# A 36-column tile placed in a dead tile's buffer, and the addresses behind it, in a decoder forward and backward kernel

## The chip, the cores and the metric

The kernel runs on one core of a Trainium2 chip. Its time is the device time of one execution in microseconds (us). Three runs gave 1169.02 us in the median (1167.36 to 1169.89).

## The reference

Four layers are applied to a residual vector `x` of two rows (batch 2, one decode position, width 1024): attention against a cache, an MLP, then the same two again with the same weights. The kernel returns the result and the gradients with respect to `x`, both caches, `wq`, `wo`, `w1`, `b1`, `w2` and `b2`.

```python
def _A_ref(x, k_cache, v_cache, wq, wo):        # 32 query heads, 4 kv heads, 16384 positions, head size 128
    ...
    q = (x @ wq).reshape(B, Sq, Hq, Dh).transpose(0, 2, 1, 3)
    k = jnp.repeat(k_cache, rep, axis=1)
    v = jnp.repeat(v_cache, rep, axis=1)
    p = _softmax(jnp.einsum("bhqd,bhkd->bhqk", q, k) * (Dh ** -0.5), axis=-1)
    o = jnp.einsum("bhqk,bhkd->bhqd", p, v)
    return o.transpose(0, 2, 1, 3).reshape(B, Sq, Hq * Dh) @ wo

def _B_ref(x, w1, b1, w2, b2):                   # 1024 -> 3584 -> 1024
    h = _gelu(jnp.einsum("bsd,df->bsf", _layernorm(x), w1) + b1)
    return jnp.einsum("bsf,fd->bsd", h, w2) + b2

x = x + _A_ref(_layernorm(x), k_cache, v_cache, wq, wo)
x = x + _B_ref(_layernorm(x), w1, b1, w2, b2)
x = x + _A_ref(_layernorm(x), k_cache, v_cache, wq, wo)
x = x + _B_ref(_layernorm(x), w1, b1, w2, b2)
...
_out, _vjp = jax.vjp(_f, A_x, A_k_cache, A_v_cache, A_wq, A_wo, B_w1, B_b1, B_w2, B_b2)
```

All inputs and outputs are bfloat16. Each cache is 2 x 4 x 16384 x 128, which is 32 MiB.

## The kernel before

The program is written as a list of pieces (`emit`), in an order fixed by hand; `Program.run` (lines 106 to 138) goes through the list and, ahead of each piece, gives free buffers to the next loads in the order of their first use. Nothing else schedules: each engine takes its instructions in the order in which the pieces issue them.

The buffers are 15 tiles called `slot0` to `slot14` (line 273), each of 128 partitions x 4096 bfloat16, so 8,192 bytes in every partition. Layer 1's tiles `e1` and `ds1` lend further buffers of the same size until they are needed for themselves. One load (`ld_kv` line 320, `ld_rows` line 325) fills one buffer, mostly 1 MiB, and is issued from SyncE's queue. A piece of a cache is 8,192 contiguous bytes in each partition; a piece of `wq`, `wo` or `w2` is four runs of 2,048 bytes; a row of `w1` is one run of 7,168 bytes.

The forward pass of both attention layers reads K and V, the backward pass of layer 1 reads them again, and so does that of layer 0. K and V blocks are turned on VectorE by 32 x 32 transposes of pairs of bfloat16 taken as int32 (line 482, into the tile `kT`) and multiplied on TensorE (lines 495 and 520). Until the backward pass of layer 0 begins at some 700 us, hardly anything is written to memory. From there on the gradients of the caches and of the weights are made as outer products (lines 1180 and 1234), cast from PSUM into halves or wholes of the slots on ScalarE (line 236) or VectorE (line 239), and stored from GpSimd's queue (lines 1185 and 1260), while K and V are still being read.

On-chip memory is taken from pools one behind the other: `const`, `vec`, `wrk`, `small`, `ktp`, `xp`, `bkp`, `pers` (lines 191 to 198). Within a pool each name takes its size rounded up to 32 bytes, times its buffers, in the order of first use. `dbias` is the last name in `wrk`, so its 144 bytes, rounded to 160, lie ahead of everything in the five pools behind: the small vectors of `small`, `kT`, `xt`, `blk`, `e0`, `e1`, `ds1`, `ds0`, `X0`, `X1` and the slots.

`dbias()` (lines 1266 to 1280) makes the gradients of `b1` and `b2`. It sums the four columns of `dh_all` and `gM_all` into the 28 + 8 columns of the tile `dbias` (lines 1271 and 1272), turns that on TensorE (line 1274), copies the rows into a half slot (line 1275) and stores them (lines 1277 and 1278). It is one piece among the background pieces of the last backward pass.

`g_a` is a tile of the same pool with two buffers of 128 x 56 float32. `gelu` takes one for each layer (line 828) and reads it last in line 848.

Of the kernel before, what the change touches and what calls it, by code (L numbers as in the profile page):

```python
# [9 lines left out]
F32 = mybir.dt.float32  # L10
# [131 lines left out]
def kernel(  # L142
# [27 lines left out]
    PE = nc.tensor  # L170
# [8 lines left out]
    DJ = D // 128  # L179
    FJ = F // 128  # L180
# [12 lines left out]
    wrk = ctx.enter_context(tc.tile_pool(name="wrk", bufs=2))  # L193
# [13 lines left out]
    def flat(t):  # L207
        return t.rearrange("p a b -> p (a b)")
# [5 lines left out]
    def ob():  # L214
        st["ob"] += 1
        return obanks[st["ob"] % 3]
# [25 lines left out]
    def dve(us):  # L242
        load_of("dve", us)
# [4 lines left out]
    identf = const.tile([128, 128], F32, name="identf")  # L248
# [1017 lines left out]
    def dbias():  # L1266
        c = P.chunk(kind="half")

        def f():
            s = wrk.tile([128, FJ + DJ], F32, name="dbias", bufs=1)  # L1270
            V.tensor_reduce(out=s[:, 0:FJ], in_=dh_all[:], axis=AX.X, op=ALU.add)
            V.tensor_reduce(out=s[:, FJ:], in_=gM_all[:], axis=AX.X, op=ALU.add)
            ps = ob()[0:FJ + DJ, 0:128]
            PE.transpose(ps, s[:], identf[:])
            V.tensor_copy(out=c.ap[0:FJ + DJ, 0:128], in_=ps)
            dve(0.7)
            GP.dma_start(out_7.rearrange("(j p) -> j p", p=128), c.ap[0:FJ, 0:128])
            GP.dma_start(out_9.rearrange("(j p) -> j p", p=128), c.ap[FJ:FJ + DJ, 0:128])

        return [(f, [c])]  # L1280
# [258 lines left out]
```

## Time and profile before

One execution was profiled. Its own time was 1169.38 us, its span from the first to the last instruction 1167.6 us.

| what | value |
|---|---|
| time of three runs, median | 1169.02 us |
| the profiled execution, time / span | 1169.38 us / 1167.6 us |
| mean granted TensorE clock | 0.862 |
| TensorE busy | 830.9 us (71%) |
| TensorE weight loads busy | 621.6 us (53%) |
| VectorE busy | 770.4 us (66%) |
| ScalarE busy | 488.8 us (42%) |
| GpSimd busy | 183.4 us (16%) |
| read from / written to HBM | 356.54 MB / 98.62 MB |
| both, over the span | 390 GB/s |

Busy time of an engine is the time in which one of its instructions ran. The DMA share is the time that packets took on the core's 16 DMA engines, divided by 16 times the stretch; packets of one engine may overlap a little, so it can be above 1. The trace also holds each DMA packet with its queue, size, start and duration. A packet here is one run of bytes moved by one DMA engine, and its duration is in whole ns. PEclk is the share of its full speed that TensorE was granted.

### The profile page before, as it was taken

What the parts mean: (1) busy time and instruction counts of PE and PEld (TensorE: products, weight loads), DVE (VectorE), ACT (ScalarE), POOL (GpSimd) and SP (SyncE); (2) the same over time, 40 slices, a digit from 0 to 9 for tenths busy, and PEclk for the clock granted to TensorE, in tenths of its full rate; (3) what the DMA queues carried; (4) which work ended last, traced back from release to release, by engine and by line L of the source; (5) the groups of instructions that cost most, each with busy time, mean ns of one, the idle gap of its engine ahead of it and who ended that gap; (6) DMA issues with size and microseconds to landing.
All of it is one profiled execution on the core that took longest, in us unless ns stands there. A gap on an engine that the chain in (4) does not pass through costs nothing. (4 is left out here: it accounts for less than half of the span.)

```text
span 1167.6 us, 34350 instructions
## 1 busy us (share of the span) xinstructions
PE 830.9 (71%) x14751; PEld 621.6 (53%) x14761; DVE 770.4 (66%) x1490; ACT 488.8 (42%) x1128; POOL 183.4 (16%) x578
## 2 busy tenths in 40 slices
PE   5665565457886546888777578879666987798875
PEld 4554564456775445777767465444333444444443
DVE  5764673269886536664656465979566977787875
ACT  0422223002423221244444206758455866676773
POOL 1000000010000000110111101423222332333341
PEclk9999999999999555577877657989887989798997
DMA  9999999989999999999999997999999999999995
GB/s 356 412 414 414 413 420 410 405 319 413 410 414 414 414 399 356 405 414 412 409 414 412 377 341 275 340 405 424 401 358 407 420 415 381 425 421 399 392 419 218
DMA packets 99636, 457.37 MB, mean 392 GB/s; under 512 B 7668, under 2 KB 11778, under 8 KB 60188
## 3 DMA queue, kind: packets, MB, share of 16 engines
q1 hardware_dynamic: 81660, 356.56, 76.6%
q0 software_dynamic: 17824, 98.63, 20.7%
q8 instruction: 115, 1.88, 0.6%
q14 instruction: 37, 0.30, 0.1%
HBM read 356.54 MB, written 98.62 MB: 390 GB/s over the span
## 5 line engine op out<-in xcount | busy, mean ns | idle before, releaser
L482 DVE STREAM_TRANSPOSE kT<-slot 128x512 int32<-128x512 int32 x480 | 322.3, 694 | 130.3 <-PE sc L495 91.1
L495 PE MATMUL sc<-qbd,kT 128*128 128x32 bf16 x4096 | 264.7, 223 | 14.4 <-DVE kT L482 11.2
L495 PEld LDWEIGHTS <-kT 128*128 128x128 bf16 x4096 | 210.5, 115 | 59.1 <-issue 27.1
L520 PEld LDWEIGHTS <-slot 128*128 128x128 bf16 x3648 | 148.4, 103 | 131.7 <-issue 48.7
L236 ACT CAST slot<-sc 128x512 bf16<-128x512 f32 x332 | 189.0, 593 | 66.2 <-PE sc L1234 32.5
L520 PE MATMUL sb<-xt,slot 128*128 128x8 bf16 x3648 | 165.9, 177 | 65.3 <-DMA slot<-in_A_v_cache_dram 28.9
L239 DVE CAST slot<-sc 128x512 bf16<-128x512 f32 x187 | 126.2, 681 | 37.2 <-PE sc L1180 18.8
L1180 PE MATMUL sc<-slot,blk 128*128 128x512 bf16 x335 | 129.6, 405 | 25.7 <-DVE slot L239 8.4
L711 ACT ACTIVATE e<-sc 128x512 bf16<-128x512 f32 x32 | 19.0, 597 | 253.9 <-DVE sc L708 182.1
L236 ACT CAST slot<-sb 128x512 bf16<-128x512 f32 x169 | 100.0, 592 | 47.6 <-PE sb L1180 27.0
L530 POOL COPY xt<-ds 32x64 int32<-32x64 int32 x368 | 84.7, 230 | 192.1 <-DVE ds L980 155.9
L402 ACT COPY slot<-tp 128x512 int32<-128x512 int32 x96 | 55.2, 586 | 139.8 <-PE tp L399 138.3
L399 PE MATMUL tp<-ident,slot 128*128 128x128 bf16 x832 | 81.4, 264 | 18.0 <-DMA slot<-in_A_wq_dram 12.0
L1180 PEld LDWEIGHTS <-blk 128*128 128x128 bf16 x512 | 45.0, 99 | 69.4 <-issue 57.3
L1180 PE MATMUL sb<-slot,blk 128*128 128x512 bf16 x170 | 68.8, 405 | 17.8 <-DVE slot L239 13.1
L399 PEld LDWEIGHTS <-slot 128*128 128x128 bf16 x832 | 66.9, 121 | 21.9 <-DMA slot<-in_A_wq_dram 12.8
L530 ACT COPY xt<-e 32x128 int32<-32x128 int32 x256 | 75.6, 295 | 3.9
L239 DVE CAST slot<-sb 128x512 bf16<-128x512 f32 x96 | 65.0, 677 | 16.6 <-DMA out_dram<-slot 7.1
L1185 POOL DMA_DIRECT2D out_dram<-slot x64 | 35.3, 551 | 215.7 <-ACT slot L236 178.8
L384 DVE STREAM_TRANSPOSE slot<-slot 128x1024 int32<-128x1024 int32 (+1 forms) x48 | 55.2, 1178 | 15.3 <-DMA slot<-in_A_wq_dram 8.1
L1234 PE MATMUL sc<-slot,X 128*128 128x512 bf16 x157 | 60.7, 407 | 5.5 <-DVE slot L239 3.3
L587 POOL TENSOR_TENSOR m_rstd<-ln_vpe,neghalf 128x2 f32<-128x2 f32 x2 | 1.4, 716 | 374.2 <-DVE ln_vpe L585 374.2
(282 smaller groups left out, 932.9 us busy)
## 6 DMA issues: line engine op xcount, KB each, us to landing
slot<-in_A_k_cache_dram SPq DMA_DIRECT2D x114, 1024.0 KB, 14.4
slot<-in_A_v_cache_dram SPq DMA_DIRECT2D x109, 1024.0 KB, 13.4
out_dram<-slot POOLq DMA_DIRECT2D x64, 1024.0 KB, 11.3
slot<-in_A_wq_dram SPq DMA_DIRECT2D x31, 1024.0 KB, 12.5
slot<-in_A_wo_dram SPq DMA_DIRECT2D x27, 1024.0 KB, 12.5
out_dram<-slot POOLq DMA_DIRECT2D x54, 512.0 KB, 12.5
slot<-in_B_w_dram SPq DMA_DIRECT2D x22, 896.0 KB, 11.0
slot<-in_B_w_dram SPq DMA_DIRECT2D x11, 1024.0 KB, 11.4
```

What stands on the lines that cost most here:

```text
L236: S.copy(out=dst, in_=src)
L239: V.tensor_copy(out=dst, in_=src)
L384: V.transpose(out=t.ap[:, h * nw * 256:(h + 1) * nw * 256].bitcast(I32).rearrange("p (w j m) -> p w j m", j=4, m=32), in_=c.ap[:, 0:4 * nc ...
L399: PE.transpose(tp[:, j * 128:(j + 1) * 128], c.ap[:, off + j * 128:off + (j + 1) * 128], ident[:])
L402: S.copy(out=d.bitcast(I32), in_=tp.bitcast(I32))
L482: V.transpose(out=kT[:].bitcast(I32).rearrange("p (w j m) -> p w j m", w=4, j=4), in_=c.ap[:, (i % 4) * 1024:(i % 4 + 1) * 1024].bitcast(I ...
L495: PE.matmul(sc[:, a0:a0 + 4, :, 2 * (i % 4) + q], lhsT=kv[:, 2 * q + w, :, e], rhs=qbd[:, g, 2 * w + e], start=(w == 0 and e == 0), stop=( ...
L520: PE.matmul(acc, lhsT=c.ap[:, n * 128:(n + 1) * 128], rhs=xv[:, i // 4, t // 2, :, 2 * (i % 4) + t % 2], start=(fresh and i == 0 and t == ...
L530: (GP.tensor_copy if on[t % len(on)] == "g" else S.copy)(out=d[32 * t:32 * t + 32, c0:c0 + cn, j, :], in_=s[32 * j:32 * j + 32, c0:c0 + cn ...
L1180: PE.matmul(ps, lhsT=hold["blk"][:, j, :], rhs=flat(qm(w)[:, (u % 2) * 4:(u % 2) * 4 + 4, :]), start=True, stop=True)
L1185: GP.dma_start((dKv if w == 0 else dVv)[g, :, c * 32:(c + 1) * 32, :], stg.ap.rearrange("p (t d) -> p t d", d=128))
L1234: PE.matmul(ps, lhsT=hold[j // 4 * 4][:, j % 4, :], rhs=Y.ap[:, y_at + c0:y_at + c0 + cn], start=True, stop=True)
```

## The change

The sums are written into a buffer of `g_a` in place of a tile of their own. The buffer has 56 columns, of which the first 36 are used.

```diff
         def f():
-            s = wrk.tile([128, FJ + DJ], F32, name="dbias", bufs=1)
+            s = flat(wrk.tile([128, FJ, 2], F32, name="g_a")[:])[:, 0:FJ + DJ]
             V.tensor_reduce(out=s[:, 0:FJ], in_=dh_all[:], axis=AX.X, op=ALU.add)
             V.tensor_reduce(out=s[:, FJ:], in_=gM_all[:], axis=AX.X, op=ALU.add)
             ps = ob()[0:FJ + DJ, 0:128]
-            PE.transpose(ps, s[:], identf[:])
+            PE.transpose(ps, s, identf[:])
```

The instructions, their order on every engine, their waits and their shapes stay as they were; two VectorE instructions and one TensorE instruction name another tile. With the tile `dbias` gone, everything in the pools behind `wrk` begins 160 bytes lower in each partition:

| tile | byte address before | after |
|---|---|---|
| `kT` (first of 3) | 36,000 = 70 x 512 + 160 | 35,840 = 70 x 512 |
| `xt` (first of 2) | 42,144 = 82 x 512 + 160 | 41,984 = 82 x 512 |
| `e0` | 49,312 = 96 x 512 + 160 | 49,152 = 96 x 512 |
| `ds1` | 82,080 = 160 x 512 + 160 | 81,920 = 160 x 512 |
| `slot0` | 104,608 = 204 x 512 + 160 | 104,448 = 204 x 512 |
| `slot14` | 219,296 = 428 x 512 + 160 | 219,136 = 428 x 512 |

All of `kT`, `xt`, `blk`, `e0`, `e1`, `ds1`, `ds0`, `X0`, `X1` and the slots had the remainder 160 and now have none. The pools `const`, `vec` and the rest of `wrk` stay in place.

## The prediction

> **What bounds the kernel now.** I read the page's slices first: is one resource full from end to end?
>
> ```profile
> DMA  9999999989999999999999997999999999999995
> GB/s 356 412 414 414 413 420 410 405 319 413 410 414 414 414 399 356 405 414 412 409 414 412 377 341 275 340 405 424 401 358 407 420 415 381 425 421 399 392 419 218
> DMA packets 99636, 457.37 MB, mean 392 GB/s; under 512 B 7668, under 2 KB 11778, under 8 KB 60188
> ...
> q1 hardware_dynamic: 81660, 356.56, 76.6%
> q0 software_dynamic: 17824, 98.63, 20.7%
> ```
>
> It is: the DMA engines are busy in nine tenths or more of almost every slice, and the two data queues fill 76.6 + 20.7 = 97.3% of the span. TensorE with 71% and VectorE with 66% have room. Second, the busy time by stretches: three stages that only load, the long last stage that loads and stores, and two short pure samples.
>
> ```profile
> core 0: us, PE busy (x) PEld busy (x) DVE busy (x) ACT busy (x) POOL busy (x), PEclk, DMA share, GB/s
> 29.00:204.00 175.00, 106.38 (x2252) 92.64 (x2250) 107.32 (x218) 48.52 (x145) 0.00 (x0) 1.00 1.02 414
> 262.00:437.00 175.00, 118.53 (x2575) 105.04 (x2576) 122.11 (x256) 47.35 (x144) 2.42 (x9) 0.85 1.02 412
> 467.00:642.00 175.00, 137.11 (x3076) 130.36 (x3074) 101.58 (x190) 72.07 (x191) 25.80 (x112) 0.74 1.02 411
> ...
> 758.00:1138.00 380.00, 303.14 (x3537) 161.91 (x3542) 289.75 (x496) 253.03 (x505) 121.77 (x354) 0.90 1.00 405
> ...
> 783.00:812.00 29.00, 26.92 (x309) 15.05 (x311) 23.91 (x42) 22.79 (x44) 8.51 (x24) 0.93 1.01 424
> 145.00:175.00 30.00, 19.96 (x424) 17.80 (x424) 20.73 (x44) 7.02 (x20) 0.00 (x0) 1.00 1.01 420
> ```
>
> The three load stages (525 us together) hold DMA at a share of 1.02 and reach 411 to 414 GB/s; where loads and stores mix, the same engines reach 424 at a share of 1.01. So time in the load stages is the time of DMA packets, and packets there are a little dearer than they need be. Third, the packets themselves, from the trace's records of size and duration. Loads of 8,192 bytes last 309 ns at the least; in the three load stages only some 10% of them do, the mean is 315.2, 315.3 and 315.8 ns and the 90th percentile 320. Loads of 2,048 bytes last 84 ns at the least, 88.0, 88.1 and 87.5 in the mean, 93 or 92 at the 90th percentile. From 758 to 1138 us, 89% of the 8,192-byte loads and 97% of the 2,048-byte ones are at 309 and 84 ns, and 91% of the 8,192-byte stores too.
>
> **The change part by part.** *The moved sums.* The four instructions of the piece that name the tile:
>
> ```profile
> L1271 DVE TENSOR_REDUCE dbias<-dh_all x1: 247/247/247, 829.1 to 829.1; 128x28 f32<-128x112 bf16 x1
> L1272 DVE TENSOR_REDUCE dbias<-gM_all x1: 164/164/164, 829.3 to 829.3; 128x8 f32<-128x32 bf16 x1
> L1274 PEld LDWEIGHTS sc<-identf,dbias x1: 96/96/96, 829.5 to 829.5; 128*36 128x36 f32 x1
> L1274 PE MATMUL sc<-identf,dbias x1: 287/287/287, 829.5 to 829.5; 128*36 128x128 f32 x1
> ```
>
> They stay with the same shapes. A wait for the old user of `g_a` could be new, but `gelu` read it last at 231.9 us (layer 0) and 449.5 us (layer 1), and the sums come at 829.1: cost nothing. Were that cover gone, the 247 + 164 ns of VectorE would be late by as much as the wait, with the K/V transposes of line 482 queued behind.
>
> *The engines' operands.* `kT`, `xt`, `e`, `ds` and the slots are read and written at new addresses by every engine. Does an engine mind where in a block of 512 bytes it begins? Line 420 answers from the trace of before, since its reads begin 160 or 416 and its writes 160, 288, 416 or 32 bytes behind a multiple of 512:
>
> ```profile
> L420 DVE STREAM_TRANSPOSE slot<-slot x28: 601/603/665, 424.7 to 454.8; 128x448 int32<-128x448 int32 x28
> L420 DVE STREAM_TRANSPOSE ds<-slot x4: 596/602/603, 425.2 to 441.0; 128x448 int32<-128x448 int32 x4
> ```
>
> A median of 603 ns with a least of 601 over all these starts: VectorE does not mind, and I put zero for it and for ScalarE and TensorE. These engines would also be covered: the load stages use 106 to 137 of 175 us of TensorE.
>
> *The transfers.* Every large load ends in a moved tile and every large store begins in one. No packet of before has a start at a multiple of 512 in these tiles, so I bound the price. The upper end of the gain within the observed packets: all that lies over the least duration goes. In the three load stages that is 20,790 packets of 8,192 bytes by 315.4 - 309 = 6.4 ns and 19,531 of 2,048 bytes by 87.9 - 84 = 3.9 ns, on 16 engines: 8.3 + 4.8 = 13.1 us. The lower end is a loss: packets could get as slow as the slowest tenth is now, 4.6 ns and 5.1 ns more: 6.0 + 6.2 = 12.2 us. Zero lies between. I take a gain, since a partial block at both ends of each 8,192-byte run is the one thing that the change removes, and the excess is per packet rather than per byte (6.4 ns on 8,192 bytes, 3.9 ns on a quarter of that), as a cost of a packet's ends would be. Not all of 13.1 us lands, because packets overlap: 525 us at 1.02 are 535.5 us of packet time; less 13.1 it is 522.4, and at the share of the mixed sample, 1.01, that takes 517 us. The gain is 8 us. The other 640 us get none: in the mixed stage loads are at the least already, and the tail from 1138 us is at a DMA share of 0.56.
>
> *The sum:* 0 + 0 - 8 against the profiled 1169.4 us: 1161 us, between 1156 (all 13.1) and 1167. That execution stands 0.4 us over the median of the three runs, so 1161 is against 1169.0 as well. What goes missing in the load stages arrives at the end whole only if SyncE finds free slots that much sooner; its largest waits before loads are for the turns,
>
> ```profile
> SPq L320 <- DVE kT L482: 177.5, 53, 11.8
> SPq L320 <- PE sc L495: 81.8, 28, 10.2
> ```
>
> and these waits lie ahead of transfers that land 13 to 14 us after their issue, so the queue is ahead of the engines and follows them when they get data earlier.
>
> **The rivals.** *B, the least duration falls too.* Packet times fit bytes plus a fixed part: (309 - 159) ns for 4,096 bytes more is 36.6 ns per 1,000 bytes, which leaves 9 ns of each 8,192-byte packet, 9 of a 4,096-byte store (159) and 9 of 2,048 bytes (84). If 160 bytes' worth of it, 5.9 ns, comes from the bytes before the start within an aligned block, then 99,636 - 7,668 = 91,968 packets by 5.9 ns on 16 engines are 33.9 us, of which some 31 would land (most stages are full): 1138 us. Against it: the 4-byte semaphore packets last 9 ns too, and their size has no room for it. Also, the 2,048-byte packets that carry eight rows of 256 bytes of `ident`, which starts 128 bytes behind a multiple of 256, last 84 ns in most cases, as one run of 2,048 does; eight starts cost no more than one. [...]
>
> *C, no change.* The excess over 309 ns comes from the HBM side of a stage that only reads. For it: the same slots at the same addresses take loads at 309 ns in 89% of cases as soon as stores run beside them, so the address alone isn't enough for an excess. Then all terms are zero: 1169 us.
>
> *D, slower.* The same term with the other sign: runs that all begin at the same place of a block meet in the on-chip memory's write side, where only loads press (the three load stages). Price as above, from the mean towards the 90th percentile, 12.2 us if all packets go there, half of it likely: 1175. It decides from the point where the mean 8,192-byte load passes 315 ns. For it: load durations lie in steps from 309 to 321 ns, so something shared does delay them. Against it: all moved tiles had one common remainder before as well (160), so they stood to each other as they will.
>
> **How the numbers follow.** Forecast 0.37; B 0.18; C 0.20; D 0.25. A measurement of this kernel can tell about 0.2% (2.3 us) from no change. Faster by more: forecast and B, 0.55. Within: C, 0.20. Slower: D, 0.25. The predicted time is the forecast's, 1161 us, with a range of its own from 1156 to 1166. To leave out no more than 2 in 10, the range takes C, most of B down to 1138, and most of D up to 1178.
>
> **What would show it.** Right: in the three load stages the share of 8,192-byte loads at 309 ns rises from a tenth to most, GB/s there from 411 to 414 towards 420, and the stages end some 8 us earlier, with the mixed stage of the same length. B: packets below 309 and 84 ns, in stores as well. C: the same packet durations. D: means above 315 ns. Wrong in another way: a change in the duration of lines 482, 236 or 495, which would mean that engines mind the start after all, or a lower granted clock in 642 to 758 us, where DMA is not full.

## The result, and the profile after

The changed kernel takes 1157.23 us in the median (1155.52 to 1158.26, four runs) against 1168.77 us (1167.36 to 1169.89, four runs of the kernel before). The ratio is 0.99 with a 95% interval of 0.9883 to 0.9918: 11.5 us or 1.0% faster. The profiled execution took 1158.26 us, its span is 1156.5 us.

The slices of the page, with the busy share of the DMA engines, the rate and the data queues:

```profile
DMA  9999999989999999999999996999999999999994
GB/s 364 421 421 423 422 426 418 406 310 419 419 421 424 422 399 367 415 418 421 418 422 420 373 368 267 349 421 422 370 382 407 418 379 405 424 421 419 398 420 180
DMA packets 99636, 457.37 MB, mean 395 GB/s; under 512 B 7668, under 2 KB 11778, under 8 KB 60188
...
q1 hardware_dynamic: 81660, 356.56, 76.4%
q0 software_dynamic: 17824, 98.63, 20.7%
```

The same packets and bytes move, and the engines are as full as before. The slices of the three load stages showed 405 to 420 GB/s and now show 415 to 426, but for one (some 404 to 437 us) that shows 399 both times. The busy time by stretches, in the same windows and columns as in the prediction:

```profile
29.00:204.00 175.00, 107.75 (x2300) 94.06 (x2299) 107.12 (x219) 48.52 (x145) 0.00 (x0) 1.00 1.02 422
262.00:437.00 175.00, 121.67 (x2716) 108.44 (x2716) 125.93 (x262) 47.37 (x144) 0.72 (x1) 1.00 1.01 417
467.00:642.00 175.00, 139.31 (x3096) 132.24 (x3093) 103.80 (x188) 73.03 (x192) 26.54 (x116) 0.72 1.02 420
642.00:758.00 116.00, 88.80 (x1509) 62.24 (x1510) 81.78 (x150) 58.49 (x125) 22.94 (x69) 0.78 0.90 338
758.00:1138.00 380.00, 301.16 (x3487) 161.67 (x3494) 285.27 (x491) 249.17 (x497) 120.47 (x352) 0.90 0.99 401
```

In the three load stages the rate rises from 414, 412 and 411 to 422, 417 and 420 GB/s at about the same DMA share (1.02 each before, 1.02, 1.01 and 1.02 after), so packets got shorter. In the last line, where stores run too, nothing is gained: 405 before, 401 after, but the changed kernel is some 12 us further in its work there, so this window takes in more of the slow end. A shorter window leaves the end out; before, then after:

```profile
758.00:1095.00 337.00, 268.12 (x3094) 142.46 (x3098) 256.76 (x442) 221.63 (x438) 106.29 (x309) 0.89 0.99 403
758.00:1095.00 337.00, 268.05 (x3074) 141.89 (x3077) 256.93 (x442) 221.76 (x437) 107.72 (x310) 0.90 1.00 405
```

The packets, from the trace's records (the least duration is the one that 99% of the loads from 29 to 642 us have after the change; under 1% are recorded 1 to 3 ns below it):

| packets | mean before | mean after | at the least duration (or below) before | after |
|---|---|---|---|---|
| 8,192-byte loads, 29 to 642 us (least 309 ns) | 315.5 ns | 310.6 ns | 11% | 99% |
| 2,048-byte loads, 29 to 642 us (least 84 ns) | 88.9 ns | 86.1 ns | 42% | 99% |
| 8,192-byte loads, 758 to 1138 us | 320.4 ns | 321.6 ns | 89% | 90% |
| 8,192-byte stores, 758 to 1138 us | 314.1 ns | 312.8 ns | 91% | 93% |

The engines' instructions did not change: the transposes of line 482 take 695 ns in the mean (694 before), the casts of line 236 take 593 ns into the slots from `sc` (593), the products of line 495 take 223 ns (223).

Where the time went is read from work that both kernels do in the same order. Line 977 is the first VectorE work of each backward half block (its first start is in layer 1), and the `sb` group of line 236 starts with the first gradient of the last layer. Before, then after; the two times ahead of the semicolon are the first and the last start:

```profile
L977 DVE TENSOR_TENSOR ds_tmp<-sc,dl x32: 651/681/693, 478.8 to 1131.0; 128x512 f32<-128x512 f32 x32
L236 ACT CAST slot<-sb x169: 569/585/685, 709.4 to 1155.6; 128x512 bf16<-128x512 f32 x169
```

```profile
L977 DVE TENSOR_TENSOR ds_tmp<-sc,dl x32: 650/682/693, 472.0 to 1119.6; 128x512 f32<-128x512 f32 x32
L236 ACT CAST slot<-sb x169: 570/586/678, 696.5 to 1144.5; 128x512 bf16<-128x512 f32 x169
```

The changed kernel is 6.8 us ahead when the backward pass of layer 1 begins and 12.9 us ahead when the first gradients are cast; 11.1 us of that are left at the last cast. From the first to the last cast it takes 448.0 us instead of 446.2.

### The profile page after: what moved, and what is told of

The parts are those of the page before. It is cut to its first block, busy times and chain, and to the rows that moved or that the text cites. A ratio compares the mean times of both kernels' runs of the same rounds, so it can differ in the third digit from the quotient of the medians.

```text
span 1156.5 us, 34350 instructions
## 1 busy us (share of the span) xinstructions
PE 829.5 (72%) x14751; PEld 620.1 (54%) x14761; DVE 770.8 (67%) x1490; ACT 488.5 (42%) x1128; POOL 183.4 (16%) x578
## 6 DMA issues: line engine op xcount, KB each, us to landing
slot<-in_A_v_cache_dram SPq DMA_DIRECT2D x109, 1024.0 KB, 12.9
```

## The experiments

The excess of a packet is its duration over the least one. Theory S: the place within a block of bytes at which a load's destination begins sets the excess of its packets. Its rivals put the cause in the engines' operands or in the stage; how large the block is was open as well. Kernels with a dead tile have the same instructions in the same order as the changed kernel or the one before.

### Which tiles

In the changed kernel, a dead tile moves only the slots back to the remainder 160:

```diff
+    pad = pers.tile([128, 40], F32, name="pad")
     slot_tiles = [pers.tile([128, CH], BF16, name=f"slot{i}") for i in range(NSLOT)]
```

> The changed kernel, with a dead tile of 160 bytes put between X1 and slot0: the slots begin at 160 past a multiple of 512 again, while kT, xt, blk, e0, e1, ds1, ds0, X0 and X1 stay at multiples. Theory S (the start of a load's destination sets the excess of its packets): 8,192-byte loads in the three load stages are at 309 ns in about a tenth of cases again, mean near 315, and the time is 1166 to 1169 us (a few loads into e1 and ds1 stay short). Rival E (the engines' operands, kT and xt above all, disturb or delay transfers when they begin off a multiple): loads stay at 309 ns, time 1157.

In the kernel before, with `dbias` in its own place, a dead tile moves only the slots to the remainder 0:

```diff
+    pad = pers.tile([128, 88], F32, name="pad")
     slot_tiles = [pers.tile([128, CH], BF16, name=f"slot{i}") for i in range(NSLOT)]
```

> The kernel before, with dbias in its own place and a dead tile of 352 bytes between X1 and slot0: only the slots begin at multiples of 512, all the rest stays at 160. Theory S: loads into slots at 309 ns in nearly all cases, 1157 to 1159 us. Rival E: as before, 1168 to 1169 us. It also tells whether the place of the sums matters: by both theories it does not.

Measured: with the slots alone at 160, 1167.69 us, ratio 0.999 to the kernel before (0.9979 to 1.0001). With the slots alone aligned, 1154.80 us, ratio 0.9887 (0.9866 to 0.9908). The stretch from 467 to 642 us of the first and of the second:

```profile
467.00:642.00 175.00, 137.68 (x3083) 130.56 (x3080) 102.01 (x190) 71.33 (x190) 25.80 (x112) 0.73 1.02 410
```

```profile
467.00:642.00 175.00, 136.09 (x3074) 129.44 (x3071) 102.95 (x185) 72.89 (x192) 26.65 (x116) 0.74 1.02 420
```

The rate follows the slots: 410 and 420 GB/s, as before and after the change. In the first kernel 28% of the 8,192-byte loads from 29 to 642 us are at 309 ns, rather than 11%. In the second it is 99%. So the start of the slots decides, the engines' tiles (`kT`, `xt`, `blk`, `X`) don't matter, and neither does where the sums of the bias gradients stand: the second kernel has the tile `dbias` as before and is as fast as the changed one.

The buffers that `e1` and `ds1` lend say more, since in both kernels they begin differently from the slots. 20 K and V loads go into them before 437 us; these are 2,560 of the 14,114 packets of 8,192 bytes that start between 29 and 437 us.

In the second kernel these 20 loads are the unaligned ones. Only 149 of all the packets in that time (1%) are off 309 ns, against 90% in the kernel before, so unaligned loads that come singly or a few in a row among aligned ones hardly pay. Taken in the order of their starts, 128 packets to a load, the first four in a row have 0, 0, 5 and 20% of their packets off 309 ns.

In the first kernel the same 20 loads are the aligned ones. There the first four have 14, 0, 0 and 1% off (packets of neighbouring loads mix in this order: at the changes from 8,192-byte to 2,048-byte loads between 29 and 437 us of the kernel before, 12 to 113 of the 8,192-byte packets start behind the first 2,048-byte one), while the five loads into slots ahead of them have 81 to 91%. Behind a later group of three, which starts at 141 us, the next five loads into slots have 1, 7, 55, 75 and 87%, over some 12 us.

So theory S holds with an addition: a load into an aligned buffer stays short among unaligned ones, but an unaligned load isn't dear by its address alone. It gets dear after some 10 us of unaligned loads, and a few aligned loads put that off again.

### Which block

As the last name of the pool `wrk` in the changed kernel, a dead tile of 256, 128 or 64 bytes, so that everything in the pools behind it moves:

```diff
             s = flat(wrk.tile([128, FJ, 2], F32, name="g_a")[:])[:, 0:FJ + DJ]
+            wrk.tile([128, 64], F32, name="pad", bufs=1)        # 32 for 128 bytes, 16 for 64
```

> The changed kernel with a dead tile of 256 bytes behind g_a's pool, so that kT, xt, e, ds, X and the slots begin 256 past a multiple of 512. If the block that matters is 512 bytes: loads at a mean near 315 ns, 1168 us. If it is 256 bytes or less: loads at 309 ns, 1157 us.

> The changed kernel with a dead tile of 64 bytes, so that everything behind begins 64 past a multiple of 512. If the block that matters is 64 bytes (160 is two and a half of them): loads at 309 ns, 1157 us. If it is 128 bytes or more: loads near a mean of 315 ns, 1168 us, perhaps with another spread than at 160.

> The changed kernel with a dead tile of 128 bytes, so that kT, xt, e, ds, X and the slots begin 128 past a multiple of 512. If the block is 128 bytes: loads at 309 ns, 1156 us. If it is 256 bytes (a remainder of 256 was as good as none, one of 64 was not): loads at a mean of 315 to 316 ns in the load stages, 1168 to 1171 us.

| remainder behind a multiple of 512 | median | ratio (95%) | 8,192-byte loads at 309 ns, 29 to 642 us | mean |
|---|---|---|---|---|
| 0 (the change) | 1157.23 us | 0.99 (0.9883 to 0.9918) | 99% | 310.6 ns |
| 256 | 1155.35 us | 0.9889 (0.9865 to 0.9912) | 99% | 310.6 ns |
| 128 | 1168.78 us | 0.9991 (0.9977 to 1.0005) | 32% | 315.2 ns |
| 64 | 1170.88 us | 1.0015 (1.0003 to 1.0026) | 9% | 315.9 ns |
| 160 (before) | 1168.77 us | 1 | 11% | 315.5 ns |

The ratios are to runs of the kernel before that were taken along; beside the remainder 128 these had 1169.93 us in the median, beside the others 1168.77. The stretch from 467 to 642 us with 256, then with 128:

```profile
467.00:642.00 175.00, 138.42 (x3074) 131.53 (x3071) 102.83 (x185) 72.96 (x192) 26.63 (x116) 0.73 1.02 420
```

```profile
467.00:642.00 175.00, 139.52 (x3082) 132.51 (x3079) 101.44 (x189) 72.58 (x191) 25.80 (x112) 0.73 1.02 411
```

The block is 256 bytes, as far as these five remainders tell: a multiple of 512 is more than is needed, one of 128 isn't enough. The steps in which the durations come depend on the remainder: of those off 309 ns, the commonest is 311 ns at 160 (30% of all packets) and 312 ns at 64 (47%).

### Why the loads beside stores were spared

Before the change, the same slots at the same remainder took loads at 309 ns late in the kernel. Two kernels leave the stores of the cache and weight gradients out, one with the slots at 160, one with them at 0:

```diff
-                        GP.dma_start((dKv if w == 0 else dVv)[g, :, c * 32:(c + 1) * 32, :], ...)
+                        pass
...
-                GP.dma_start(out_ap[...], ap[:, 0:rb * cn].rearrange("p (j n) -> p j n", j=rb))
+                pass
```

> The kernel before without the stores of lines 1185 and 1260: the gradients of both caches and of the four weight matrices are made and cast into the slots, but not written to memory. The slots keep the remainder of 160. Theory N (the excess needs a load packet whose neighbours on its DMA engine are loads too; stores between them hide it): from 760 us to the end, where before 89% of the 8,192-byte loads were at 309 ns, a tenth to a third are, with a mean 4 to 6 ns above 309. Rival H (the excess belongs to what the early stages read or how fast they read, not to the absence of stores): the late loads stay at 309 ns. The time is a little shorter than 1169 us, as engines then set the late stage; no theory gives it exactly.

> The changed kernel without the same stores, as a control for the last: by both theories nearly all late loads are at 309 ns, and the early stages are those of the changed kernel.

Measured, with one profiled execution each: 1126.56 us at 160 and 1111.63 us at 0. The late stage, at 160 and at 0:

```profile
758.00:1095.00 337.00, 290.85 (x3504) 155.74 (x3500) 287.17 (x495) 251.19 (x502) 57.99 (x247) 0.95 0.58 210
```

```profile
758.00:1095.00 337.00, 289.89 (x3469) 156.55 (x3467) 281.79 (x489) 247.48 (x495) 57.61 (x247) 0.95 0.54 195
```

DMA is busy in little more than half of the stretch (0.58 and 0.54), since TensorE (290.85 and 289.89 of 337 us busy) and VectorE (287.17 and 281.79) now set its pace. At 160, 79% of the late 8,192-byte loads are at 309 ns, at 0 it is 85%. That is neither the tenth to a third of theory N nor a clear yes to rival H, and with the aligned slots it is fewer than the nearly all that were expected. The loads now come in short bursts, so the packets were sorted by how long at least 14 of the 16 DMA engines had been busy (gaps under 0.02 us not counted), from 690 us on and without the packets of 330 ns or more:

```
time since the run     slots at 160                        slots at 0
of transfers began     packets   at 309 ns   mean          packets   at 309 ns
1 to 2 us              1928      98%         309.1 ns      1891      98%
4 to 6 us               505      95%         309.3 ns       623      99%
8 to 12 us              471      85%         309.8 ns       488      98%
12 to 20 us             814      49%         311.5 ns       361      100%
20 to 40 us             387       9%         313.7 ns       253      100%
```

Late loads do get the excess, in full, once a run of unaligned loads has lasted 20 us, and with the aligned slots they don't; rival H falls. In the kernel before, with stores among them, the loads from 690 us on that come more than 40 us into a run are at 309 ns in 96% of cases. The late excess costs no time where the engines set the pace: of the 14.9 us between these two kernels, 14.6 are there when the first gradients are cast (709.8 and 695.2 us).

Three kernels of transfers alone took the engines out altogether. Two of them issue 256 loads of K and V pieces into the 15 slots in turn, the third 128 loads, each followed by a store. A dead tile ahead of the slots, which the lines below leave out, puts them at 160 or at 0, and the kernel ends behind the loop:

```diff
+    for rep in range(4):                     # 2 in the third
+        for g in range(G):
+            for c in range(NCH):
+                for src, dst in ((Kv, dKv), (Vv, dVv)):
+                    t = slot_tiles[n % NSLOT]
+                    n += 1
+                    nc.sync.dma_start(t[:].rearrange("p (t d) -> p t d", d=128), src[g, :, c * 32:(c + 1) * 32, :])
+                    GP.dma_start(dst[...], t[:].rearrange(...))       # in the third alone
```

> Only loads: 256 K and V pieces of 1 MiB go into the 15 slots in turn, the slots at 160 past a multiple of 512; all computation and all stores are left out. Theory P (the excess is made among the DMA engines themselves, when packets that begin and end within a 256-byte block follow each other in a long run of loads): after the first 10 to 20 us some 10% of the packets are at 309 ns and the mean is near 314 ns, as in the load stages. Rival Q (it comes from the engines that read and write the on-chip memory at the same time): with the engines idle nearly all packets are at 309 ns.

> The same 256 loads with the slots at multiples of 512. Theory P: nearly all packets at 309 ns, and the whole shorter than with 160 by 5 ns of 309 per packet, some 1.5% of about 650 us, which is 10 us, or a little less as packets overlap. Rival Q: the same time and durations as with 160.

> 128 loads into the slots at 160, each followed by a store of the slot to a gradient's place; all computation is left out, so these outputs hold the caches. Theory N (stores between the loads hide the excess): loads are at 309 ns in 85% to 95% of cases in runs as long as one likes. Without N: at 309 ns in some 10% as with the loads alone.

Measured, again with one profiled execution each; the lines are a stretch of 200 us from the middle. Here only VectorE, GpSimd, the clock, the DMA share and the rate are listed, since the other engines do nothing. Loads at 160, loads at 0, loads at 160 with stores:

```profile
130.00:330.00 200.00, 0.00 (x0) 0.00 (x0) 1.00 1.01 422
```

```profile
130.00:330.00 200.00, 0.00 (x0) 0.00 (x0) 1.00 1.01 427
```

```profile
130.00:330.00 200.00, 0.00 (x0) 21.78 (x41) 1.00 1.01 427
```

| kernel | time | loads at 309 ns | mean of the loads | stores at 309 ns |
|---|---|---|---|---|
| loads, 160 | 643.11 us | 13% | 314.2 ns | |
| loads, 0 | 634.61 us | 99.8% | 309.3 ns | |
| loads and stores, 160 | 636.88 us | 98.6% | 310.3 ns | 99.7% |

Theory P holds and rival Q falls: with idle engines the excess is the same, 4.9 ns per packet, and alignment takes it away, 8.5 us of 643 (1.3%). It also sets in late: at 160 all packets between 5 and 10 us after the first are at 309 ns, half of those between 10 and 20 us, and a constant 11% from then on. Theory N's outcome came too, and more fully than the 85% to 95% that were expected: with as many stores among them, loads at 160 stay at 309 ns for the whole 635 us. In this kernel the slots are also written at half the rate of the first (134.23 MB of loads in a span of 635.1 us rather than 268.45 MB in 641.3), so that the stores themselves do it is not shown.

## Why the prediction was right, step by step

**What bounds the kernel.** Right. The three stages with most of the gain are those where DMA was at a share of 1.02. TensorE's clock did not decide: the profiled executions of the changed kernel and of the one with the remainder 128 both had 0.897 in the mean, at spans of 1156.5 and 1167.1 us. From 262 to 437 us the latter had a clock of 1.00 and 412 GB/s, and the kernel with the slots alone aligned 0.56 and 417 GB/s.

**The moved sums and the engines' operands: zero.** Right, and shown: the kernel with `dbias` in its old place and aligned slots has the whole gain, and the one with aligned engine tiles and unaligned slots has none that can be told from zero.

**The transfers: a gain of 8 us.** The cause was right, and the term was too small. It was a choice more than a result: no packet of the kernel before had an aligned start in these tiles, so its own trace could not tell a gain from a loss, and the 0.37 said so. The argument for the gain, a cost of each packet's two ends, holds only in part. An aligned start does take the excess away, but the excess is no fixed price of a packet: in the kernel of loads alone at 160 all packets between 5 and 10 us after the first are at 309 ns, and with 20 unaligned loads among aligned ones 1% of the packets are off it.

The size missed in two places. First, I gave up 5 of 13.1 us to overlap by taking the DMA share down from 1.02 to 1.01, whereas two of the three stages stayed at 1.02. What did not go was something else, a few long packets (after the change 180 in the three stages, 26 to 874 ns over their least duration, 3.1 us in all): the time above the least duration, over packets of 8,192, 7,168 and 2,048 bytes and on 16 engines, fell from 13.2 to 3.2 us in the three stages. By the rates these stages gained 525 x (1 - 412.3 / 419.7) = 9.2 us. Second, I gave nothing to the rest of the time before 700 us (0 to 29, 204 to 262, 437 to 467, 642 to 700), where loads run alone too. Counting only packets within 25 ns of the least duration, the excess was 10.4 us in the three stages and 2.5 us in the rest before the change, and under 0.1 us in both after it. That is 12.8 us less packet time, and the lead at the first cast is 12.9 us. One reading was slightly off, and touches only the bound of the loss: in the second stage the 90th percentile of the 8,192-byte loads is 319 ns rather than 320.

**The rest gets nothing.** Right for the mixed stage. The 1.8 us that it took longer after the change are no new cost that can be shown: from the first to the last cast of this group, the two other aligned kernels of the same computation took 447.0 and 446.9 us, and the unaligned ones between 446.2 and 447.8.

**The rivals.** B, a lower least duration, did not happen: it is 309 and 84 ns before and after the change, and stores that read the slots at 160 are at 309 ns in 99.7% of cases. No run shows the 5.9 ns that B put on every packet with an unaligned start: reads of unaligned slots pay nothing, and writes into them pay only in long runs of unaligned loads (at 160, 13% of the packets are at 309 ns with loads alone and 98.6% with stores among them). C rested on the loads at 309 ns beside stores; that row was real, and the three kernels of transfers show why it misled: with stores among the loads 98.6% are at 309 ns at 160, and without them the address decides (13% at 160, 99.8% at 0). D, the same term with the other sign, fell with the first profile.

**What stays open.** Why the excess needs 10 to 20 us of unaligned loads to appear, and why stores or aligned loads among them keep it away, isn't settled; the records don't say which engine moved a packet. How the excess depends on a packet's size (6.4 ns on 8,192 bytes against 3.9 on 2,048 in the prediction) was not tested on its own.

## What to carry to other kernels

Where loads bind, look at the duration of single DMA packets against their least, and at the byte address of every buffer that loads write: here a start at a multiple of 256 bytes was worth 1.0% to 1.1%, and a small tile allocated ahead of the buffers can take it away. A dead tile of 352 bytes gave it back without touching the rest of the code. A stage that mixes loads and stores can be free of the effect, as here (89% of the late 8,192-byte loads at 309 ns before the change), and so can one in which only some of the buffers are unaligned (99% with the slots alone aligned); a row that looks clean there is no proof for a stage of unaligned loads alone.

## What the runs showed of the hardware that was not expected

The effect is a matter of time as much as of address: at a remainder of 160, loads alone ran at the least duration for some 10 us and then settled at 314 ns for good, and where three loads into aligned buffers came between, the next unaligned one had 99% of its packets at 309 ns again. And the order of the remainders isn't what the number of bytes off would suggest: 64 was no better than 160 (1170.88 us and 1168.77 us), and 128, with 32% of the loads at the least duration, gained nothing that can be measured (ratio 0.9991, 0.9977 to 1.0005).
